# Another planned instruction order for a fused attention and two-layer-pair kernel on one core

## The chip, the cores and the metric

The kernel runs on one core of a Trainium2 chip. The metric is the device time of one execution in microseconds (us). A program that this kernel writes for itself decides at build time in which order each engine's instructions stand; the change gives that program other numbers.

## The reference, cut to what matters

All inputs are drawn at random; attention has 4 batches, 8 heads, 768 steps and a head size of 48, so 3072 tokens of width 384.

```python
def _attn_ref(q, k, v, alpha):
    for t in range(S):
        state = alpha[:, :, t, :, None] * state + np.einsum('bhd,bhe->bhde', k[:, :, t], v[:, :, t])
        y[:, :, t] = np.einsum('bhd,bhde->bhe', q[:, :, t], state)
def _moe_ref(x, w_in, w_out):          # w_in 384x2048, w_out 2048x384
    h = x @ w_in
    g = h * np.cos(h)
    return (g @ w_out).astype(np.float32)
def _moe2_ref(x, w1, w2, w3, w_out):   # w1, w2, w3 384x768, w_out 768x384
    h = np.maximum(np.maximum(x @ w1, x @ w2), x @ w3)
    return (h @ w_out).astype(np.float32)
```

The output is `_moe2_ref` of `_moe_ref` of the attention's result.

## The kernel before

**Tiling.** The 3072 tokens are six units of 512. Every unit goes through attention in four parts (pairs of heads, `k` = 0 to 3), then through the first pair of layers in 16 steps, one for each 128 of the 2048 hidden columns, so 96 steps in all (`moe1(i)`), and, after all units, through the second pair of layers. `att0` is the attention of unit 0, `att` that of units 1 to 5. In `att`, POOL scales k (L505) and q (L508) by running products of alpha that DVE makes with scans (L501, L506); TensorE (PE) transposes k (L513), makes the products of q and k and of k and v (L525, L529), and later the attention's values (L559, L566).

**Products of high and low parts.** PE multiplies fp32r numbers. Each operand is therefore split into a high part and a low part, and each product is three matmuls: L604 to L606 for `x @ w_in` (three such groups in a step, one for each 128 rows of x) and L631 to L633 for `g @ w_out` (three groups, one for each third of the output columns). In a step, ACT and DVE take turns between them: ACT rounds h to a whole number of turns (L612), DVE takes the turns off (L613), ACT takes the sine (L614), DVE multiplies by h (L616 in the first four steps, L620 later), ACT writes the high part (L617, L621), and the low part is a subtraction, on POOL (L618) in the first four steps and on DVE (L626) later. The bank of PSUM that held h is free after the product (first four steps) or after L626. There are five such banks for everything but the three output sums `acc`.

**Weights.** `weight` brings a block of 128x384 weights, stored with 8 bytes each, by a DMA (L344) into one of four buffers `raw` and makes a high and a low part of it: ACT takes the exponents (L345), DVE shifts and joins (L346), ACT writes the high part (L350), and the low part is a subtraction. Where the block's number modulo 4 is in `LOD`, L346 writes a PSUM bank, `raw` is free after it, and DVE subtracts (L352); elsewhere L346 writes back into `raw`, and POOL subtracts (L354). For the first pair of layers even blocks are of `w_in` (tiles `wih`, `wil`), odd ones of `w_out` (`woh`, `wol`); there are 16 of each.

**End of a unit.** The three sums `acc` leave through the one buffer `yy1`, one after the other: ACT copies the high part (L640), DVE subtracts (L641), and a DMA writes both to memory (L643, `x1d`). The copy of the next sum waits until that DMA has landed.

**What sets the order.** Nothing is put into the engines' queues directly. `op` records every step with its engine, an estimated duration, what it reads and writes, and a due number; `Program.order` then plays all engines against each other and, whenever an engine is free, takes the recorded step with the smallest due number among those that it holds to be ready. The due numbers count in steps of the first pair of layers: `moe1(i)`'s matmuls are due at `i`, weights `W1E` steps ahead of their use, their loads `early` before that, attention's part `k` of unit `u` at `16 (u - 1) + ATT0 + ATTS k`. Each engine then executes its queue strictly in that order, SP's queue of DMAs among them. Where the played PE is idle between 7.5 and 45 us, `tile_kernel` fills in matmuls on the identity (L843).

Lines of the planner that the change touches: when a load counts as landed, when its users are ready, and (in `dma_w`) how long weights occupy the DMA:

```python
dma_free = max(dma_free, end + (0.65 if e == "SP" else 1.05)) + nbytes / 295e3
end = dma_free + 0.9
ready_at[u] = max(ready_at[u], end + lag)
return nbytes * 295.0 / 400.0
```

Of the kernel before, what the change touches and what calls it, by code (L numbers as in the profile page):

```python
# [26 lines left out]
P = 128  # L27
C = 64
HB = 512
# [7 lines left out]
KO = AL + 2  # L37
# [6 lines left out]
PR = 112  # L44
# [12 lines left out]
LIMIT = {"h": 3, "a": 3, "t": 2, "w": 1, "r": 2, "y": 2, "r0": 2, "s0": 2}  # L57


RYS = 1  # L60


GLE1 = 0
GLP1 = 4


XLE = 1
MKP = 0
GATE, GSTEP = 1, 3
LOD = (0, 2)  # L70

W1E = 12
MOE_EARLY = 5
EARLY = 3
FIRST = -12
ATT0 = -4.0
ATTS = 3.6


WARM, COLD, IDLE = 2.45, 7.0, 2.5  # L80
# [2 lines left out]
class Program:  # L83
# [38 lines left out]
    def order(self, banks, limit):  # L122
        n = len(self.ops)
        left = [len(o[4]) for o in self.ops]
        users = [[] for _ in range(n)]
        for i, o in enumerate(self.ops):
            for d in o[4]:
                users[d].append(i)
        opens = {}
        bank_of = [[] for _ in range(n)]  # L130
        open_left = {}
        for k, v in self.of_bank.items():
            opens.setdefault(min(v), []).append(k)
            open_left[k] = len(v)
            for i in v:
                bank_of[i].append(k)
        bank_free = [0.0] * banks
        freed_at = {c: [0.0] * limit[c] for c in limit}
        bank_end = {}
        chosen = {}  # L140
        engines = sorted({o[0] for o in self.ops})
        free = dict.fromkeys(engines, 0.8)
        waiting = {e: [] for e in engines}
        ready_at = [0.0] * n
        for i in range(n):
            if not left[i]:
                waiting[self.ops[i][0]].append(i)
        start, ended = [0.0] * n, [0.0] * n
        dma_free = 0.0
        port_free = 0.0  # L150
        cold = COLD
        mode = False
        issued, block, fetched = 0, BLOCK, 0.0
        never = float("inf")

        def single(t):
            return min(range(banks), key=lambda m: (bank_free[m] > t, bank_free[m], m))

        def ready(i):
            t = ready_at[i]  # L160
            need = opens.get(i, ())
            if need:

                t = max(t, sorted(freed_at[need[0][1]])[len(need) - 1], sorted(bank_free)[len(need) - 1])
            if self.ops[i][6]:
                t = max(t, port_free)
            return t

        for _ in range(n):
            _, e, t = min((t - (0.1 if e == "Pool" else 0.0), e, t) for e, t in (  # L170
                (e, max(free[e], min(map(ready, w)))) for e, w in waiting.items() if w))
            assert t < never
            i = min((self.ops[j][5], j) for j in waiting[e] if ready(j) <= t)[1]
            waiting[e].remove(i)
            _, dur, nbytes, _, _, _, port, tiled, count = self.ops[i]
            start[i] = t
            if e == "PE":
                if tiled != mode:
                    dur += SWITCH
                    mode = tiled  # L180
                if t - free[e] > IDLE:
                    cold = t + COLD
                dur += min(dur, max(0.0, cold - t) / 2)
                issued += count
                if issued >= block:
                    late = max(0.0, fetched - t - dur * (1.0 - (issued - block) / count))
                    dur += late
                    fetched = t + dur + (FETCH[1] if dma_free > t + dur else FETCH[0])
                    block += BLOCK
            free[e] = t + dur  # L190
            end = t + dur
            if port:
                port_free = end
            if nbytes is not None:
                dma_free = max(dma_free, end + (0.65 if e == "SP" else 1.05)) + nbytes / 295e3
                end = dma_free + 0.9
            ended[i] = end
            for k in opens.get(i, ()):
                f = min(range(limit[k[1]]), key=lambda f: freed_at[k[1]][f])
                m = single(t)  # L200
                chosen[k] = m
                bank_end[k] = (m, f, 0.0)
                freed_at[k[1]][f] = never
                bank_free[m] = never
            for k in bank_of[i]:
                m, f, last = bank_end[k]
                last = max(last, end + self.SEM)
                bank_end[k] = (m, f, last)
                open_left[k] -= 1
                if not open_left[k]:  # L210
                    freed_at[k[1]][f] = last
                    bank_free[m] = last
            for u in users[i]:
                lag = self.LAG.get((e, self.ops[u][0]), self.SEM)
                ready_at[u] = max(ready_at[u], end + lag)
                left[u] -= 1
                if not left[u]:
                    waiting[self.ops[u][0]].append(u)
        self.start, self.end = start, ended
        return sorted(range(n), key=lambda i: (start[i], i)), chosen  # L220
# [32 lines left out]
def dma(nbytes):  # L253
    return max(nbytes, 15e3)


def dma_w(nbytes):
    return nbytes * 295.0 / 400.0


HW = 0.46


@with_exitstack
def tile_kernel(ctx, tc, aa, qk, vv, wt, outT):
    nc = tc.nc
# [62 lines left out]

    raw_n = [0]  # L330

    def weight(block, hi, lo, whi, wlo, due, extra=(), early=2.0):
        r, tn = (raw_n[0] % NRAW1, raw_n[0] % NTOP) if block < NW1 else (raw_n[0] % NRAW, 0)
        raw_n[0] += 1
        raw, rk, top, tk = raw_b[r], ("raw", r), top_b[tn], ("top", tn)
# [17 lines left out]
        else:  # L353
            op("Pool", pool(WB), lambda: ge.tensor_tensor(lo(), w, hi().bitcast(F32), ALU.subtract), [wk, whi], [wlo], due)  # L354

    def weight1(f, kind, due, early=2.0):
        t = wi if kind == "i" else wo

        def part(n):
            return t[n][:, f].rearrange("p k n -> p (k n)") if kind == "i" else t[n][:, f]  # L360

        weight(2 * f + (kind == "o"), lambda: part("h"), lambda: part("l"), (f"w{kind}h", f), (f"w{kind}l", f), due, early=early)
# [118 lines left out]
    def att(u, k, p, t0):  # L481
        m = u * NP + k
        n2, na, nk, nv = m % 2, m % NIN, m % NKQ, m % NV
        t, kq_, v, kt, a, s, d, z, iv = al_b[na], kq_b[nk], v_b[nv], kt_b[n2], a_b[n2], s_b[p], d_b[n2], z_b[n2], inv0[n2]
        vk, kk_ = ("v", nv), nk
# [6 lines left out]
        kf, kk, kq = ("inf", na), ("ink", kk_), ("inq", kk_)  # L492
# [1 line left out]
        sk = [("s", p, j) for j in range(2)]  # L494
        half = [slice(UP * h, UP * h + D) for h in range(2)]
        first = t0
        op("SP", HW, lambda: nc.sync.dma_start(t, aa[u, p, :, 0:KO]), (), [kf], first - 4.8 + (0.8 if not k else 0), dma(PR * KO * 4))
        op("SP", HW, lambda: nc.sync.dma_start(kq_, qk[u, p]), (), [kk, kq], first - 3.9, dma(PR * 2 * HB * 4))
        op("SP", HW, lambda: nc.sync.dma_start(v, vv[u, p]), (), [vk], first - 3.7, dma(P * HB * 3))
        gate = [("wil", GATE + GSTEP * k)] if u == 1 else []  # L500
        op("DVE", 0.07 + 0.00208 * AL, lambda: ve.tensor_tensor_scan(  # L501
            gf[:, ::-1], t[:, 1:AL + 1][:, ::-1], one0.rearrange("p c t -> p (c t)"), 0.0, ALU.mult, ALU.add), ["one0", kf, *gate], [(*kg, 0), (*kg, 1)], t0 - 1, port=True)
# [49 lines left out]

        yks, y = psum2("r" if u <= RYS else "y")

# [24 lines left out]
        for h in range(2):  # L579
            cs = slice(HB // 2 * h, HB // 2 * (h + 1))  # L580
            first = xa and p == 0 and h == 0
# [232 lines left out]
    start, end = G.start, G.end  # L814
# [9 lines left out]
    for i in order:  # L824
        t = start[i]
# [91 lines left out]
```

## Time and profile before

| | |
|---|---|
| three executions, median (lowest to highest) | 788.72 us (787.69 to 791.11) |
| the profiled execution | 792.77 us |
| its span, first to last instruction | 790.8 us |
| PE busy in the span | 772.0 us |
| DVE, ACT, POOL busy | 427.0, 347.6, 124.3 us |
| granted clock of TensorE, share of full speed | 1.00 |

The profile is of one execution: each instruction with its engine, start and duration, and for an engine that sat idle, what ended the idle time. The durations of neighbouring matmuls overlap, since PE takes the next one up before the last one is through; from start to start a 512-column matmul takes about 0.23 us though each is shown as 0.39. The profiled execution lies 4.05 us above the median of the three others.

### The profile page before, as it was taken

To read this page: it belongs to the slowest core of one execution; us is meant where nothing else is said; L and a number is where in the kernel's file an instruction comes from. 1 tells how busy PE (TensorE), PEld (TensorE's weight loads), DVE (VectorE), ACT (ScalarE), POOL (GpSimd) and SP (SyncE) were. 2 spreads that over 40 slices of the span, in tenths; PEclk is the share of its full clock that TensorE was granted. 3 is DMA by queue.
4 is the path that set the end of the run, shared out by engine and by line. 5 is a ranking of instruction groups with operands and counts; after the bars stand their busy time and mean duration, and the time that the engine had idled before them with its cause. 6 is when DMAs were issued, how large, how long until landed. Compare 5 with 4: busy or idle time off the path is not lost. (4 is left out here: it accounts for less than half of the span.)

```text
span 790.8 us, 14190 instructions
## 1 busy us (share of the span) xinstructions
PE 772.0 (98%) x5863; PEld 625.4 (79%) x5863; DVE 427.0 (54%) x720; ACT 347.6 (44%) x669; POOL 124.3 (16%) x133
## 2 busy tenths in 40 slices
PE   7899899999999999999999999999999999999998
PEld 6677677888888888888878788888888888888886
DVE  8778899756875786566467555532222322223221
ACT  4778756455644554555577444511111212112111
POOL 4463442111111111121133000300000000000000
PEclk9999999999999999999999999999999999999999
DMA  9867735121321133012246300611020200200001
GB/s 276 249 195 205 219 92 164 54 53 47 133 77 29 46 133 94 1 39 107 53 141 225 115 0 2 218 53 42 27 80 27 73 34 28 80 27 14 14 27 41
DMA packets 26464, 69.84 MB, mean 88 GB/s; under 512 B 3392, under 2 KB 6464, under 8 KB 26400
## 3 DMA queue, kind: packets, MB, share of 16 engines
q1 hardware_dynamic: 26400, 68.93, 27.6%
q8 instruction: 46, 0.75, 0.4%
q14 instruction: 18, 0.15, 0.1%
HBM read 52.80 MB, written 14.16 MB: 85 GB/s over the span
## 5 line engine op out<-in xcount | busy, mean ns | idle before, releaser
L631 PE MATMUL acc<-gh,woh 128*128 128x512 f32 x288 | 116.8, 405 | 2.8 <-DVE yy L641 2.4
L604 PE MATMUL ps<-xt,wih 128*128 128x512 f32 x288 | 114.8, 399 | 1.8 <-DVE q L616 1.0
L633 PE MATMUL acc<-gl,woh 128*128 128x512 f32 x288 | 113.1, 393 | 2.5 <-DVE gl L626 2.5
L632 PE MATMUL acc<-gh,wol 128*128 128x512 f32 x288 | 112.5, 391 | 0.0
L606 PE MATMUL ps<-xt,wil 128*128 128x512 f32 x288 | 112.4, 390 | 0.1
L605 PE MATMUL ps<-xt,wih 128*128 128x512 f32 x288 | 112.3, 390 | 0.0
L613 DVE SCALAR_TENSOR_TENSOR q<-q,ps 128x512 f32<-128x512 int32 x96 | 65.4, 682 | 52.5 <-ACT q L612 52.4
L626 DVE TENSOR_TENSOR gl<-ps,gh 128x512 fp32r<-128x512 f32 x92 | 63.2, 687 | 38.5 <-ACT gh L621 38.2
L612 ACT ACTIVATE q<-ps 128x512 int32<-128x512 f32 x96 | 56.8, 595 | 58.5 <-PE ps L606 58.4
L620 DVE TENSOR_TENSOR ps<-q,ps 128x512 f32<-128x512 f32 x92 | 63.6, 691 | 34.8 <-ACT q L614 34.5
L692 DVE TENSOR_TENSOR ps<-t,ps 128x512 f32<-128x512 f32 x36 | 25.1, 696 | 103.5 <-PE ps L684 103.5
L614 ACT ACTIVATE q<-q 128x512 f32<-128x512 f32 x96 | 60.4, 630 | 46.4 <-DVE q L613 46.2
L621 ACT ACTIVATE gh<-ps 128x512 fp32r<-128x512 f32 x92 | 54.7, 594 | 44.3 <-DVE ps L620 38.7
L693 ACT ACTIVATE h<-ps 128x512 fp32r<-128x512 f32 x36 | 21.6, 599 | 108.0 <-DVE ps L692 107.9
L633 PEld LDWEIGHTS acc<-gl,woh 128*128 128x128 f32 x288 | 54.0, 188 | 17.4 <-DVE gl L626 5.4
L631 PEld LDWEIGHTS acc<-gh,woh 128*128 128x128 f32 x288 | 54.0, 188 | 16.2 <-DVE yy L641 3.7
L604 PEld LDWEIGHTS ps<-xt,wih 128*128 128x128 f32 x288 | 54.0, 188 | 14.3 <-DVE q L616 1.1
L606 PEld LDWEIGHTS ps<-xt,wil 128*128 128x128 f32 x288 | 54.1, 188 | 12.3 <-DVE wil L352 0.9
L690 DVE TENSOR_TENSOR t<-t,ps 128x512 f32<-128x512 f32 x36 | 24.8, 688 | 70.4 <-PE ps L684 69.7
L605 PEld LDWEIGHTS ps<-xt,wih 128*128 128x128 f32 x288 | 54.1, 188 | 10.4
L632 PEld LDWEIGHTS acc<-gh,wol 128*128 128x128 f32 x288 | 54.1, 188 | 9.7
L710 ACT ACTIVATE y<-ps 128x512 f32<-128x512 f32 x18 | 10.8, 600 | 93.2 <-PE ps L707 93.2
(147 smaller groups left out, 1425.1 us busy)
## 6 DMA issues: line engine op xcount, KB each, us to landing
raw<-in_wt SPq DMA_DIRECT2D x56, 384.0 KB, 3.9
kq<-in_qk SPq DMA_DIRECT2D x22, 448.0 KB, 4.5
x1d<-yy SPq DMA_DIRECT2D x18, 512.0 KB, 3.4
xt<-x1d SPq DMA_DIRECT2D x18, 512.0 KB, 4.5
al<-in_aa SPq DMA_DIRECT2D x23, 228.4 KB, 2.6
outT<-y SPq DMA_DIRECT2D x18, 256.0 KB, 2.0
v<-in_vv SPq DMA_DIRECT2D x23, 192.0 KB, 4.8
xt<-yy SPq DMA_DIRECT2D x30, 64.0 KB, 3.7
```

The source lines that it names most:

```text
L604: pe.matmul(ps, wi["h"][:, f, cc], xt[:, cc, 0], start=(cc == 0), stop=False)
L605: pe.matmul(ps, wi["h"][:, f, cc], xt[:, cc, 1], start=False, stop=False)
L606: pe.matmul(ps, wi["l"][:, f, cc], xt[:, cc, 0], start=False, stop=(cc == NR - 1))
L612: op("Act", act(HB, True), lambda: se.activation(q.bitcast(I32), ps, AF.Copy, bias=0.25, scale=INV2PI), [hk], [qk, *qx], m)
L613: op("DVE", dve(HB), lambda: ve.scalar_tensor_tensor(q, q.bitcast(I32), -TWOPI, ps, ALU.mult, ALU.add), [hk], [qk], m)
L614: op("Act", act(HB), lambda: se.activation(q, q, AF.Sin, bias=0.5 * math.pi), (), [qk], m)
L620: op("DVE", dve(HB), lambda: ve.tensor_tensor(ps, q, ps, ALU.mult), [qk], [hk], m)
L621: op("Act", act(HB, True), lambda: se.activation(gh, ps, AF.Copy), [hk], [("gh", gn)], m)
L626: op("DVE", dve(HB), lambda: ve.tensor_tensor(gl, ps, gh.bitcast(F32), ALU.subtract), [hk, ("gh", gn)], [("gl", gn)], m)
L631: pe.matmul(acc[c], oh, gh, start=(f == 0), stop=False)
L632: pe.matmul(acc[c], ol, gh, start=False, stop=False)
L633: pe.matmul(acc[c], oh, gl, start=False, stop=(f == NF1 - 1))
```

## The change

The planner's numbers change, and three of its rules. A load counts as landed 1.6 us after its bytes instead of 0.9. A load that `att` issues (alpha, q with k, v) counts as allowed only 5 us after the buffer that it fills is seen free (`SLACK`; the planner knows such loads by `tiled=True`, a mark that DMAs did not carry), so it takes a later place among SP's loads; nothing in the program waits those 5 us. A block of weights counts with its full bytes. The weights of the first pair of layers are due 6 steps ahead of their use instead of 12, their elementwise work and loads also later in terms of due numbers, and attention's parts of units 1 to 5 later and closer together. `LOD` moves DVE's subtraction from PSUM from `w_in` to `w_out`: the low part of `w_in` is now POOL's, that of `w_out` DVE's. `GSTEP` lets unit 1's scans start after other blocks of `w_in`. `XLE` makes the low part of the first three parts of unit 0's attention by a matmul and an ACT copy (L476, L477), where it was only the first; two DVE subtractions (L479) go. `RYS` lets the values of all units share the two banks of the products. The filling matmuls L843 fall away, as the played PE has no such gap any more.

```diff
-RYS = 1
+RYS = 9
...
-XLE = 1
+XLE = 3
 MKP = 0
-GATE, GSTEP = 1, 3
-LOD = (0, 2)
-
-W1E = 12
-MOE_EARLY = 5
-EARLY = 3
-FIRST = -12
-ATT0 = -4.0
-ATTS = 3.6
+GATE, GSTEP = 1, 2
+LOD = (1, 3)
+
+W1E = 6
+MOE_EARLY = 3
+EARLY = 1
+FIRST = -4
+ATT0 = -1
+ATTS = 3.3
...
-                end = dma_free + 0.9
+                end = dma_free + LANDED
...
-                ready_at[u] = max(ready_at[u], end + lag)
+                ready_at[u] = max(ready_at[u], end + lag + (SLACK if self.ops[u][7] and self.ops[u][2] is not None else 0.0))
...
 def dma_w(nbytes):
-    return nbytes * 295.0 / 400.0
-
-
-HW = 0.46
+    return nbytes
+
+
+HW, LANDED, SLACK = 0.46, 1.6, 5.0
...
-    def weight(block, hi, lo, whi, wlo, due, extra=(), early=2.0):
+    def weight(block, hi, lo, whi, wlo, due, extra=(), early=EARLY):
...
-    def weight1(f, kind, due, early=2.0):
+    def weight1(f, kind, due, early=EARLY):
...
-        op("SP", HW, lambda: nc.sync.dma_start(kq_, qk[u, p]), (), [kk, kq], first - 3.9, dma(PR * 2 * HB * 4))
+        op("SP", HW, lambda: nc.sync.dma_start(kq_, qk[u, p]), (), [kk, kq], first - 3.9, dma(PR * 2 * HB * 4), tiled=True)
```

The last line stands for the three loads of `att`.

**PE, around the first L525 of unit 1** (`ident` alone is a filling matmul; `ps_99` to `ps_103` are the five banks). Before, all nine groups L604 to L606 of steps 0 to 2, and the filling, stand ahead of it; from the last group on:

```order
L604 MATMUL ps_99<-xt_324,wih 128x512
L605 MATMUL ps_99<-xt_324,wih 128x512
L606 MATMUL ps_99<-xt_324,wil 128x512
L843 MATMUL ps_102<-ident 128x512
L525 MATMUL ps_100<-kq_104 64x64
```

With the change:

```order
L604 MATMUL ps_102<-xt_326,wih 128x512
L605 MATMUL ps_102<-xt_326,wih 128x512
L606 MATMUL ps_102<-xt_326,wil 128x512
L525 MATMUL ps_103<-kq_104 64x64
L525 MATMUL ps_100<-kq_104 64x64
```

The bank `ps_102` there is step 1's: the three groups of step 2 now follow L525 and L529, and nothing fills.

**DVE, up to the first L626** (the low part of step 4's g; `raw0` to `raw3` and `ps0` to `ps4` are buffers and banks, `wil` and `wol` low parts of weights). Before:

```order
L620 TENSOR_TENSOR ps0_99<-q_82,ps0_99 128x512
L346 SCALAR_TENSOR_TENSOR ps4_103<-raw2_91,top0_93 128x384
L506 SCALAR_TENSOR_TENSOR al2_128<-al2_128,inv1_125 112x520
L352 TENSOR_TENSOR wil_78<-ps4_103,wih_77 128x384
L626 TENSOR_TENSOR gl0_85<-ps0_99,gh0_83 128x512
```

With the change:

```order
L620 TENSOR_TENSOR ps4_103<-q_82,ps4_103 128x512
L346 SCALAR_TENSOR_TENSOR ps3_102<-raw1_90,top1_94 128x384
L346 SCALAR_TENSOR_TENSOR raw2_91<-raw2_91,top0_93 128x384
L626 TENSOR_TENSOR gl0_85<-ps4_103,gh0_83 128x512
L352 TENSOR_TENSOR wol_80<-ps3_102,woh_79 128x384
L613 SCALAR_TENSOR_TENSOR q_82<-q_82,ps1_100 128x512
L506 SCALAR_TENSOR_TENSOR al2_128<-al2_128,inv1_125 112x520
```

The scan L506 and a weight's subtraction L352 stood ahead of L626 and now follow it.

**POOL, around the q of unit 1's last part** (L508; `wol` and `wil` are the low parts of `w_out` and `w_in`). Before:

```order
L354 TENSOR_TENSOR wol<-raw_90,woh 128x384
L539 TENSOR_TENSOR d_112<-s_119,g_130 112x192
L354 TENSOR_TENSOR wol<-raw_92,woh 128x384
L508 TENSOR_TENSOR kq_105<-kq_105,al_127 112x512
L546 COPY kq_105<-kq_105 48x256
```

With the change:

```order
L505 TENSOR_TENSOR kq_105<-kq_105,g_130 112x512
L539 TENSOR_TENSOR d_112<-s_119,g_130 112x192
L508 TENSOR_TENSOR kq_105<-kq_105,al_127 112x512
L354 TENSOR_TENSOR wil<-raw_89,wih 128x384
L546 COPY kq_105<-kq_105 48x256 x2
L354 TENSOR_TENSOR wil<-raw_91,wih 128x384
```

The last two subtractions of weights stood ahead of L508 and now follow it; on DVE the scan L506 that feeds this L508 now stands well ahead of the last L346 of the weights, where it stood behind it.

## Rows read from the trace of the kernel before

**Rows 1.** The page, part 1: busy time of each engine
```profile
PE 772.0 (98%) x5863; PEld 625.4 (79%) x5863; DVE 427.0 (54%) x720; ACT 347.6 (44%) x669; POOL 124.3 (16%) x133
```
**Rows 2.** Stages: width, busy PE, PEld, DVE, ACT, POOL (instructions), clock, DMA share, GB/s
```profile
0.00:26.00 26.00, 21.58 (x182) 16.89 (x183) 21.41 (x46) 14.16 (x36) 14.01 (x23) 1.00 0.96 275
26.00:60.00 34.00, 30.13 (x256) 21.96 (x255) 26.11 (x46) 24.02 (x50) 17.25 (x17) 1.00 0.66 213
60.00:100.00 40.00, 35.96 (x431) 27.52 (x434) 35.76 (x68) 31.45 (x66) 17.64 (x20) 1.00 0.71 205
100.00:140.00 40.00, 39.04 (x565) 30.89 (x556) 38.97 (x69) 23.91 (x49) 13.70 (x14) 1.00 0.43 126
140.00:400.00 260.00, 260.00 (x2757) 211.13 (x2756) 169.98 (x296) 138.85 (x270) 41.17 (x40) 1.00 0.23 68
400.00:440.00 40.00, 38.36 (x166) 30.01 (x165) 28.32 (x46) 30.40 (x59) 14.46 (x14) 1.00 0.61 199
440.00:787.00 347.00, 346.96 (x1531) 286.96 (x1529) 106.49 (x157) 84.25 (x142) 6.12 (x6) 1.00 0.13 47
```
**Rows 3.** PE's timeline: start, duration, instruction [idle before it, ended by]
```profile
25.83 0.39 PE L604 MATMUL ps<-xt,wih 128*128 128x512 f32 x1
...
30.54 0.50 PE L604 MATMUL ps<-xt,wih 128*128 128x512 f32 x1 [0.57 <-ACT wih L350]
...
35.47 1.02 PE L843 MATMUL ps<-ident 128*128 128x512 f32 x2
...
38.80 0.50 PE L604 MATMUL ps<-xt,wih 128*128 128x512 f32 x1 [1.03 <-DVE q L616]
...
59.60 0.51 PE L633 MATMUL acc<-gl,woh 128*128 128x512 f32 x1 [1.52 <-DVE gl L626]
...
80.16 0.50 PE L633 MATMUL acc<-gl,woh 128*128 128x512 f32 x1 [0.99 <-DVE gl L626]
...
99.38 0.69 PE L525 MATMUL ps<-kq 48*64 48x64 f32 x32 [2.25 <-POOL kq L508]
...
135.71 0.50 PE L631 MATMUL acc<-gh,woh 128*128 128x512 f32 x1 [0.96 <-DVE yy L641]
...
437.81 0.50 PE L631 MATMUL acc<-gh,woh 128*128 128x512 f32 x1 [1.46 <-DVE yy L641]
```
**Rows 4.** ACT's and DVE's timeline before the wait that ended at 59.60
```profile
57.39 0.65 ACT L345 ACTIVATE top<-raw 128x384 f16<-128x384 bf16 x1 [1.36 <-DMA raw<-in_wt]
...
58.39 0.56 DVE L352 TENSOR_TENSOR wil<-ps,wih 128x384 fp32r<-128x384 f32 x1 [1.45 <-ACT wih L350]
```
**Rows 5.** DVE's and POOL's timeline before the wait that ended at 99.38
```profile
94.98 0.56 DVE L346 SCALAR_TENSOR_TENSOR raw<-raw,top 128x384 uint32<-128x384 uint32 x1 [1.36 <-ACT top L345]
95.46 1.24 DVE L506 TENSOR_TENSOR_SCAN al<-al,inv 112x520 f32<-112x520 f32 x1
...
97.18 1.01 POOL L354 TENSOR_TENSOR wol<-raw,woh 128x384 fp32r<-128x384 f32 x1 [4.43 <-ACT woh L350]
98.15 1.17 POOL L508 TENSOR_TENSOR kq<-kq,al 112x512 f32<-112x512 f32 x1
```
**Rows 6.** Groups by line: busy us, mean ns | idle before, releasers
```profile
L476 PE MATMUL acc<-yy,gl 128*128 128x512 f32 x1 | 0.5, 487 | 0.0
...
L352 DVE TENSOR_TENSOR wil<-ps,wih 128x384 fp32r<-128x384 f32 x16 | 8.8, 549 | 2.6 <-ACT wih L350 2.4
...
L354 POOL TENSOR_TENSOR wol<-raw,woh 128x384 fp32r<-128x384 f32 x16 | 17.4, 1086 | 28.8 <-ACT woh L350 23.6 <-DMA al<-in_aa 2.4 <-issue 2.2
```
**Rows 7.** The page, part 6: loads of weights, KB each, median us from issue to landing
```profile
raw<-in_wt SPq DMA_DIRECT2D x56, 384.0 KB, 3.9
```
**Rows 8.** One stretch, L604 alone: width, busy PE, PEld (instructions), clock, DMA share, GB/s
```profile
36.00:99.00 63.00, 13.52 (x33) 6.19 (x33) 1.00 0.68 204
```
**Rows 9.** DVE's and POOL's timeline at 46 us
```profile
45.98 1.34 DVE L346 SCALAR_TENSOR_TENSOR ps<-raw,top 128x384 uint32<-128x384 uint32 x1
...
45.87 1.02 POOL L354 TENSOR_TENSOR wol<-raw,woh 128x384 fp32r<-128x384 f32 x1
```

More of the change, by code (lines that the diff above doesn't have):

```diff
@@ L496, in att @@
         first = t0
-        op("SP", HW, lambda: nc.sync.dma_start(t, aa[u, p, :, 0:KO]), (), [kf], first - 4.8 + (0.8 if not k else 0), dma(PR * KO * 4))
-        op("SP", HW, lambda: nc.sync.dma_start(kq_, qk[u, p]), (), [kk, kq], first - 3.9, dma(PR * 2 * HB * 4))
-        op("SP", HW, lambda: nc.sync.dma_start(v, vv[u, p]), (), [vk], first - 3.7, dma(P * HB * 3))
+        op("SP", HW, lambda: nc.sync.dma_start(t, aa[u, p, :, 0:KO]), (), [kf], first - 4.8 + (0.8 if not k else 0), dma(PR * KO * 4), tiled=True)
+        op("SP", HW, lambda: nc.sync.dma_start(kq_, qk[u, p]), (), [kk, kq], first - 3.9, dma(PR * 2 * HB * 4), tiled=True)
+        op("SP", HW, lambda: nc.sync.dma_start(v, vv[u, p]), (), [vk], first - 3.7, dma(P * HB * 3), tiled=True)
         gate = [("wil", GATE + GSTEP * k)] if u == 1 else []
```

## The prediction

> **What bounds the kernel now.** I first read the busy times of the page [rows 1]: PE is busy 772.0 of 790.8 us. The reader is to see two things there. No change of order can win more than the other 18.8 us as long as PE's own work stays, and the 54% of DVE say nothing, since they are a mean over a crowded start and an empty end.
>
> So the second view is busy time by stage [rows 2]. PE's idle time is the width less its busy time: 4.42 us before 26, 3.87 from 26 to 60, 4.04 from 60 to 100, 0.96 from 100 to 140, nothing from 140 to 400, 1.64 from 400 to 440, nothing after; the 3.8 after 787 are the last result's way out. Two stretches, 607 us long, have a full PE whatever the order. Of what a new order can win, 7.9 us lie between 26 and 100, and there DVE and ACT are nearly full too: from 60 to 140 DVE is busy 74.7 of 80 us, PE 75.0. The clock is at its upper level, 2.4 GHz, in every stage, so nothing is to be had from it.
>
> The third view is PE's timeline, for the single waits and what ended each [rows 3]: 0.57 for a weight, 1.03 for a bank that L616 frees, 1.52 and 0.99 for a low part by L626, 2.25 for a q that POOL scales, 0.96 and 1.46 for the end of a unit. Besides, 1.02 us of PE's busy time at 35.47 is filling.
>
> The fourth is the timelines of the engines that were waited for. Before 59.60 ACT waited 1.36 us for a load, and so DVE 1.45 for L352, and L626, which had its inputs, stood behind it [rows 4]. Before 99.38 DVE waited 1.36 us with L346 for a load; the scan L506, which does not need that weight, stood behind, and on POOL L508 stood behind a weight's L354 which had waited 4.43 [rows 5]. Both are work blocked behind a weight's load that it doesn't need.
>
> **The change, part by part.** The sum is made against the profiled execution, 792.77 us, which is 4.05 above the median, 788.72.
>
> *Start, +0.7 us.* PE gets two more L476, 0.49 each as shown [rows 6], 0.23 from start to start, and each then waits for ACT's copy of the high part; DVE loses two subtractions, which PE did not wait for. PE's values of unit 0's first part also move ahead of the second part's products of q and k, and wait there for DVE's masks: in the old order PE had done something else meanwhile. The two L476 alone are 0.46, with nothing beside them on PE; the reordering costs up to one more product of that kind. Bounds 0 and 1.5; I take 0.7, so the first L604 comes at about 26.5 instead of 25.83.
>
> *26 to 60, -3.6 us.* The filling, 1.02, is not emitted. The wait of 0.57 was for step 2's weights; its groups now follow L525 and L529, which give ACT and POOL 0.69 us and more, so it goes. The wait of 1.03 was for step 0's bank: the same chain L612, L613, L614, L616 is left, with about as much PE work beside it, so I count half of it, 0.5. The 1.52 go: L626 stands ahead of L352 and of L506, and behind two L346, whose loads are the ones to watch. The rest of the stage's 3.87, some 0.75 in single waits up to 0.4, I leave as it is. 1.02 + 0.57 + 0.5 + 1.52 = 3.6. Bounds: 4.9 if all of it goes, 2.0 if L626 is then held up by a load in L346.
>
> *60 to 100, -2.25 us.* The long wait goes: L506 stands well ahead of the last L346, and POOL's L508 ahead of the last two L354. Its chain has then no weight in it. The other 1.8 us of the stage I leave: a PE that gets through earlier asks a DVE that has 2.2 us of slack per 20 for the same work, so what is not blocked by a load is late by work. Bounds 0 and 4.04.
>
> *The low part of the weights, 0.* Sixteen times L352, 0.549, leaves the way of `w_in` and L354, 1.086, takes its place; the reverse holds for `w_out` [rows 6]. No engine has more to do. It is 0.54 us more from a load to a ready `wil`, and a buffer `raw` of `w_in` is held through L350 and L354. This is covered while one round of such a buffer (issue to landing 3.9 [rows 7], L345 0.65, L346 0.56, L350 about 0.5, L354 1.09, so 6.7) is shorter than the two steps of PE that it serves. From 36 to 99 us PE began 33 groups with L604, three to a step [rows 8], so a step lasts 63 / 11 = 5.7 us there; 11.4 us stand for the 6.7, and 4.7 are left for queues. If that cover goes, see the second rival.
>
> *End of units, -0.3 us.* The wait at 437.81 has two more groups of L604 to L606 (six starts of 0.23, 1.4 us) ahead of it, but the next sum's copy L640 now stands behind L614 and L612 of later steps, about 1.1 us of ACT. The net is -0.3. At 135.71 there is likewise more PE work ahead, and the first L641 stands behind a scan of attention, 1.24 as in [rows 5]: 0. Bounds for both together: -2.4 and +1.5.
>
> *Later units, 0.* Attention of units 2 to 5 comes later and shares two banks; from 140 to 400 PE is never idle and DVE has 90 us free [rows 2]. If a unit's last part came late, PE would stop at the unit's first L604; in the new order over 30 groups of three matmuls, 0.7 us each, stand between the two.
>
> The sum is 0.7 - 3.6 - 2.25 - 0.3 = -5.45 us: 787.3 for an execution like the profiled one, **783.3 us** for the median. A measurement of this kernel can tell about 0.5% (3.9 us) from no change; this is 0.7%.
>
> **A rule weighed.** At 45.98 a DVE L346 took 1.34 us; POOL's L354 had begun at 45.87 and ran 1.02 [rows 9]. The same operation takes 0.56 where POOL is idle [rows 5]. So a collision costs 0.78 here.
>
> The Trainium skill, SBUF — State Buffer, section "SBUF: two separate sides", says that VectorE and GpSimd hold one port pair as an exclusive lock, so that an operation of VectorE with two SBUF inputs waits for the whole of GpSimd's. The trace agrees: that L346 ended 0.43 us after the L354 did. By the rule a new order that lays L354 and L346 side by side more often loses 0.78 us each time, which is the third rival below.
>
> **The rivals.**
>
> *DVE or the loads bound the start.* For it: from 60 to 140 DVE has as much to do as PE, and DMAs are busy 96% before 26 and 66 to 71% up to 100 [rows 2]. Then what the order frees comes back as other waits of the same engines, L626 late by work or by another load. Against it: the waits named were blocked by loads that the waiting work did not need. It keeps the filling and the half of the long wait, 1.02 + 1.1, less 0.7 at the start: -1.4, 787.3 us.
>
> *`wil` becomes the last to come (slower).* L354 stands in POOL's queue among L505, L508 and L539, and the weights are due six steps later, so there is less store of ready ones. It decides where a round of a `w_in` buffer passes the 11.4 us of two steps, that is, where its 6.7 meet more than 4.7 us of queues; waits of L354 of 4.43 occur [rows 5]. Its price is then the 0.54 in each of steps 4 to 15, 12 x 0.54 = 6.5 us, with none of the waits removed but the filling's 1.02 and with the 0.7 at the start: 788.7 + 6.5 - 0.3, 795 us.
>
> *The port.* The 16 L354 move among more scans and L346. If eight of them collide anew, 8 x 0.78 = 6.2 us of DVE, where DVE has no slack: against the -5.45 it leaves +0.8, 789.5 us. Against it: there are as many L354 as before, and such collisions are in the trace already.
>
> *The order hardly matters.* PE's rows are nearly the same; if the same loads are late in the same places, the time is 788.7 within 1.5 us. Against it: the two places where the order is what blocked [rows 4, 5].
>
> **How the numbers follow.** Forecast 0.57 (778.8 to 785.6), DVE or loads 0.21 (785 to 788.7), `wil` 0.11 (790 to 797), the port 0.05, order indifferent 0.06. The lower end of the forecast is the sum with the better bounds in part (-4.9, -4.04 and -1 for the ends of units: -9.9, 778.8); its own upper end has 2.0 and 1.5 in place of 3.6 and 2.25 (-3.1, 785.6). Leaving out most of `wil` and a little on both sides gives 778.5 to 790. Faster by over 0.5% (under 784.8) takes nearly all of the forecast: 0.55. Slower by over 0.5% (above 792.7) is `wil` and a little of the rest: 0.11. Within 0.5%: 0.34.
>
> **What would show it.** Right: PE's idle time from 26 to 100 falls from 7.9 to about 4 us, no L843, no wait above 1 us at the first L633 of step 4 nor at unit 1's last L525, the first L604 at 26 to 27, and the stretches from 140 on as long as before. DVE's rivalry would show as new waits of PE for L626 or L620 between 60 and 140 with DVE above 95% busy; `wil` as waits of L606 or L604 for POOL's L354; the port as L346 or L506 of 1.2 to 2 us beside L354. I am wrong if PE's idle time by stage stays and the time falls all the same, or if units 2 to 5 show idle PE.

## The result, and the profile after

The changed kernel takes 780.73 us (median of 4 runs, 780.38 to 781.45), the kernel before 789.72 in the same measurement (4 runs, 787.69 to 791.11): a ratio of 0.989, 95% interval 0.987 to 0.991, so 9.0 us faster, 1.1%. The prediction was 783.3 in 778.5 to 790. The profiled execution took 780.58 us, close to its median; that of before, at 792.77, lay 3 us above its own. From profile to profile the difference is therefore 12.1 us of span (790.8 to 778.7), while the medians give the change 9.0.

The page, part 1, of the changed kernel answers to [rows 1]:

```profile
PE 768.0 (99%) x5863; PEld 627.5 (81%) x5863; DVE 425.1 (55%) x718; ACT 348.4 (45%) x671; POOL 127.3 (16%) x133
```

The stages of the changed kernel, with the columns of [rows 2]:

```profile
0.00:26.00 26.00, 22.83 (x188) 18.39 (x189) 21.96 (x47) 14.58 (x37) 15.14 (x24) 1.00 0.97 286
26.00:60.00 34.00, 32.22 (x332) 25.43 (x331) 29.15 (x51) 27.69 (x57) 20.20 (x20) 1.00 0.66 211
60.00:100.00 40.00, 40.00 (x478) 32.38 (x477) 38.67 (x74) 32.35 (x68) 18.68 (x21) 1.00 0.68 209
100.00:140.00 40.00, 39.02 (x469) 31.16 (x467) 34.41 (x62) 23.33 (x48) 9.76 (x10) 1.00 0.36 112
140.00:400.00 260.00, 259.03 (x2754) 210.88 (x2753) 170.75 (x296) 139.06 (x269) 42.98 (x40) 1.00 0.23 68
400.00:440.00 40.00, 39.96 (x175) 32.31 (x174) 28.35 (x46) 30.80 (x58) 14.45 (x14) 1.00 0.66 227
```

PE's timeline of the changed kernel: the rows that answer to [rows 3], with every wait of 0.2 us or more after 26 us but one (0.97 at 358.69, told below under later units):

```profile
24.75 0.40 PE L604 MATMUL ps<-xt,wih 128*128 128x512 f32 x1
...
30.30 0.50 PE L604 MATMUL ps<-xt,wih 128*128 128x512 f32 x1 [0.77 <-ACT xt L474]
31.58 0.50 PE L605 MATMUL ps<-xt,wih 128*128 128x512 f32 x1 [0.78 <-DVE xt L479]
34.22 0.50 PE L604 MATMUL ps<-xt,wih 128*128 128x512 f32 x1 [0.23 <-DVE wol L352]
36.40 0.39 PE L604 MATMUL ps<-xt,wih 128*128 128x512 f32 x1
...
124.41 0.50 PE L631 MATMUL acc<-gh,woh 128*128 128x512 f32 x1 [0.98 <-DVE yy L641]
```

What to see in the stages: PE's idle time is 3.17 us before 26 (4.42 before), 1.78 from 26 to 60 (3.87), nothing from 60 to 100 (4.04), and 0.04 from 400 to 440 (1.64). Between 34.3 and 124 us no wait of PE stands on the timeline at all. Against that, 0.97 is new between 140 and 400. Idle time falls by 8.0 us in all (sum of the stages), and PE's *busy* time falls too, from 772.0 to 768.0, of which the filling L843 is 1.0.

One line of the waits of ACT carries the explanation to which the runs lead. It gives the engine, what it waited for, the total in us, the number of waits and the longest one. Before:

```profile
ACT top L345 <- DMA raw<-in_wt: 15.0, 18, 2.5
```

and with the change:

```profile
ACT top L345 <- DMA raw<-in_wt: 4.8, 5, 1.5
```

L345 is the first of a weight block's operations. Before, ACT reached eighteen of them ahead of the block's load and stood still for 15.0 us in all, with everything behind them in its queue; now five, for 4.8 us.

### The profile page after: what moved, and what is told of

The parts are those of the page before. It is cut to its first block, busy times and chain, and to the rows that moved or that the text cites. A ratio compares the mean times of both kernels' runs of the same rounds, so it can differ in the third digit from the quotient of the medians.

```text
span 778.7 us, 14199 instructions
## 1 busy us (share of the span) xinstructions
PE 768.0 (99%) x5863; PEld 627.5 (81%) x5863; DVE 425.1 (55%) x718; ACT 348.4 (45%) x671; POOL 127.3 (16%) x133
## 4 chain that ended last, share of the span: by engine, by line
PE 94%; DMA 3%; ACT 1%; DVE 1%; issue 0%; POOL 0%; SPq 0%; ACTq 0%; POOLq 0%; DVEq 0%
PE ps L682 9%; PE ps L683 9%; PE ps L684 9%; PE acc L631 9%; PE ps L604 8%; PE acc L633 8%; PE acc L632 8%; PE ps L605 8%; PE ps L606 8%; PE ps L705 3%; PE ps L707 3%; PE ps L706 3%; PE ps L525 2%; PE ps L559 1%; DMA raw<-in_wt 1%; PE ps L566 1%
## 5 line engine op out<-in xcount | busy, mean ns | idle before, releaser
L631 PE MATMUL acc<-gh,woh 128*128 128x512 f32 x288 | 116.0, 403 | 1.0 <-DVE yy L641 1.0
L604 PE MATMUL ps<-xt,wih 128*128 128x512 f32 x288 | 114.7, 398 | 1.0 <-ACT xt L474 0.8
L633 PE MATMUL acc<-gl,woh 128*128 128x512 f32 x288 | 112.2, 390 | 0.0
L606 PE MATMUL ps<-xt,wil 128*128 128x512 f32 x288 | 112.1, 389 | 0.0
L613 DVE SCALAR_TENSOR_TENSOR q<-q,ps 128x512 f32<-128x512 int32 x96 | 65.6, 683 | 46.9 <-ACT q L612 46.8
L620 DVE TENSOR_TENSOR ps<-q,ps 128x512 f32<-128x512 f32 x92 | 63.7, 692 | 35.8 <-ACT q L614 35.7
L626 DVE TENSOR_TENSOR gl<-ps,gh 128x512 fp32r<-128x512 f32 x92 | 62.9, 687 | 35.6 <-ACT gh L621 35.0
L614 ACT ACTIVATE q<-q 128x512 f32<-128x512 f32 x96 | 60.6, 631 | 39.7 <-DVE q L613 39.4
L621 ACT ACTIVATE gh<-ps 128x512 fp32r<-128x512 f32 x92 | 54.8, 597 | 47.4 <-DVE ps L620 44.0
L631 PEld LDWEIGHTS acc<-gh,woh 128*128 128x128 f32 x288 | 54.0, 188 | 13.5 <-DVE yy L641 1.6
L604 PEld LDWEIGHTS ps<-xt,wih 128*128 128x128 f32 x288 | 54.1, 188 | 13.0 <-ACT xt L474 1.2
L633 PEld LDWEIGHTS acc<-gl,woh 128*128 128x128 f32 x288 | 54.1, 188 | 12.0 <-DVE gl L626 0.4
L606 PEld LDWEIGHTS ps<-xt,wil 128*128 128x128 f32 x288 | 54.1, 188 | 11.4
```

The lines of the kernel that those rows point to most:

```text
L604: pe.matmul(ps, wi["h"][:, f, cc], xt[:, cc, 0], start=(cc == 0), stop=False)
L606: pe.matmul(ps, wi["l"][:, f, cc], xt[:, cc, 0], start=False, stop=(cc == NR - 1))
L613: op("DVE", dve(HB), lambda: ve.scalar_tensor_tensor(q, q.bitcast(I32), -TWOPI, ps, ALU.mult, ALU.add), [hk], [qk], m)
L620: op("DVE", dve(HB), lambda: ve.tensor_tensor(ps, q, ps, ALU.mult), [qk], [hk], m)
L626: op("DVE", dve(HB), lambda: ve.tensor_tensor(gl, ps, gh.bitcast(F32), ALU.subtract), [hk, ("gh", gn)], [("gl", gn)], m)
L631: pe.matmul(acc[c], oh, gh, start=(f == 0), stop=False)
```

## The experiments

Each kernel was timed against the kernel before on the same chip; before's median lay between 789.2 and 790.5 us beside them. The changed kernel was timed only once, in the first measurement, so a difference to it of up to 1 us says nothing. The waits of L345 are those of the one profiled execution.

| kernel | median (us) | ratio to before, 95% | waits of L345 for a load (us, times) |
|---|---|---|---|
| before | 789.72 | | 15.0, 18 |
| the change | 780.73 | 0.987 to 0.991 | 4.8, 5 |
| before, three operations moved | 790.88 | 0.999 to 1.003 | 14.6, 16 |
| change, loads planned as before | 791.34 | 1.000 to 1.004 | 13.6, 12 |
| change, weights due 12 steps ahead | 785.71 | 0.993 to 0.997 | 6.8, 9 |
| change, low parts as before | 783.11 | 0.989 to 0.994 | 4.2, 4 |
| before, new rules on loads alone | 784.16 | 0.990 to 0.994 | 9.9, 9 |
| change, no hold on attention's loads | 784.26 | 0.991 to 0.994 | 6.1, 6 |
| change, landing and bytes as before | 787.36 | 0.996 to 0.998 | 14.0, 14 |
| change, end of unit 0 moved | 780.47 | 0.986 to 0.990 | 4.2, 5 |
| change, twelve L345 earlier | 793.14 | 1.002 to 1.005 | 13.2, 11 |
| change, longer landing, hold of 8 us | 793.94 | 1.004 to 1.008 | 4.2, 7 |
| change, attention due as before | 782.29 | 0.988 to 0.993 | 5.1, 5 |
| change, eight L345 earlier | 789.81 | 0.998 to 1.002 | 12.8, 10 |

**The named waits, undone by hand.** In the kernel before, L626 of step 4 goes ahead of L506 and L352, unit 1's last L506 ahead of the last L346, and L508 ahead of the last L354; nothing else.

```diff
+    for i, j in ((400, 294), (434, 259), (435, 261)):
+        order.remove(i)
+        order.insert(order.index(j), i)
```

> The order of before with three steps moved by hand and nothing else: DVE's L626 of step 4 ahead of the scan L506 and the weight's L352, DVE's scan L506 of unit 1's last part ahead of the last L346, POOL's L508 of that part ahead of the last L354. Theory (work blocked behind a weight's load): PE's waits of 1.52 us at the first L633 of step 4 and of 2.25 us at unit 1's last L525 both fall below 0.5 us, and the time falls by 2.5 to 3.8 us. Rival (DVE's work is the bound): the waits come back as others of PE between 60 and 140, and the time falls by 0 to 1.5 us.

790.88 us against 789.62: no gain, or by the interval 0.7 us at most, where 2.5 to 3.8 were expected. The waits for L626 and L508 that were named are gone, but PE's timeline of this run has others in their place:

```profile
61.28 0.69 PE L525 MATMUL ps<-kq 48*64 48x64 f32 x32 [1.25 <-POOL kq L508]
64.85 0.49 PE L604 MATMUL ps<-xt,wih 128*128 128x512 f32 x1 [0.93 <-DVE wil L352]
```

So the two places on which the largest terms of the prediction rested do not make the time. ACT's waits at L345 are hardly touched (14.6 us). PE's idle time from 26 to 100 us is lower in this one profile, 4.9 us against 7.9, but the profile of before is of an execution 3 us above its median, and in this one PE was late at the start already (first L604 at 28.20), with the granted clock at its lower level from 14.35 to 17.76 us.

**The loads' rules taken back.**

```diff
-HW, LANDED, SLACK = 0.46, 1.6, 5.0
+HW, LANDED, SLACK = 0.46, 0.9, 0.0
...
-    return nbytes
+    return nbytes * 295.0 / 400.0
```

> The changed kernel with the planner's three old rules on loads (landing 0.9, no hold on attention's loads, weights at 295/400 of their bytes). If the gain rests on the planner knowing the loads, most of it goes: 4 to 9 us slower than the changed kernel, with new waits of PE behind L345's or L346's wait for a load. If it rests on the due numbers and the low parts, 0 to 2 us slower.

791.34 us, 10.6 more than the change: with the three rules on loads gone, the whole gain is gone, though due times, low parts and the start are those of the change. ACT waits 13.6 us at L345 again. PE stood for 2.54 us until 38.39, for a bank that L616 frees.

**Due times and low parts taken back**, one at a time.

```diff
-W1E = 6
+W1E = 12
...
-EARLY = 1
+EARLY = 2.0
```

> The changed kernel with weights due 12 steps ahead and their loads 2 ahead, as before. Theory (weights that are not yet needed stood ahead of what PE waits for): 3 to 7 us slower than the changed kernel, PE idle from 26 to 100 again 4 us or more. Rival (the low parts or the rules on loads did it): within 1.5 us of the changed kernel.

785.71 us, 5.0 more than the change; L508 is waited for again (1.12 us before 60.13).

```diff
-LOD = (1, 3)
+LOD = (0, 2)
```

> The changed kernel with the low part of w_in on DVE from PSUM and that of w_out on POOL, as before. Rival (a buffer of w_out is free earlier, so loads flow earlier): 2 to 6 us slower than the changed kernel. Theory (the sum counts this as 0): within 1.5 us of it.

783.11 us, 2.4 more than the change; the intervals of the two ratios overlap, the times of the two kernels do not. ACT's waits are as short as with the change (4.2 us), and so the low parts seem to have an effect of another kind: PE waits 1.57 us before 37.63 for a bank that L616 frees. The parts are not additive: the three taken back cost 10.6, 5.0 and 2.4 us, 18.0 together, twice the change's 9.0.

**The loads' rules alone**, in the kernel before (the lines of the second run the other way round, and `tiled=True` on attention's loads). This expectation and three below describe the rule `SLACK` wrongly: it is no distance between a load's landing and its first user, but keeps attention's own loads back by 5 us in the plan.

> The kernel before with the three rules on loads alone (a load's landing planned 0.7 us later, the whole of a weight's bytes on the wire, 5 us between a landing and its first user, attention's loads under the same rule); due times, low parts, products of the start and attention's times as before. New theory, from the traces of the four runs so far: what the change wins is ACT's waits at a weight's L345 for its load, since everything in ACT's and DVE's order stands behind them. They were 15.0 us in 18 waits before, 14.6 in 16 with three operations moved by hand, 13.6 in 12 with the loads planned as before, and 4.8 in 5 with the whole change. It expects here 4 to 8 us of such waits and a time of 782 to 785.5, since due times and low parts measured 5.0 and 2.4 us. Rival (the rules need the new due times and attention's new times to have room): waits of L345 above 10 us and a time of 788 to 791. My first theory, which counted single waits of TensorE, has no reason for a gain beyond the waits at L633 and L525, about 3.8 us: 785 to 787.

784.16 us, 5.4 less than before (789.51 beside it): the rules give six tenths of the gain by themselves. The time is as the new theory expected, though only 0.8 us below the range of the first theory, and the waits (9.9 us in 9) lie above the new theory's 4 to 8.

**The two halves of the loads' rules.** First `SLACK = 0.0` alone, then `LANDED = 0.9` and 295/400 of the bytes with the 5 us kept.

> The changed kernel without the 5 us that the planner puts between a load's landing and its first user (0 in their place); landing and bytes as changed. If this distance is what takes L345 out of the way of loads that are late, ACT's waits at L345 come back above 10 us and the time is 788 to 791. If the longer landing and the whole bytes carry it, the waits stay at 4 to 7 us and the time at 781 to 783.

> The changed kernel with the load's own price as before (0.9 us to land, 295/400 of a weight's bytes), and the 5 us to the first user kept. The mirror of the run without the 5 us: if the distance carries the gain, 781 to 783 with ACT's waits at L345 at 4 to 7 us; if the price of the load carries it, 786 to 791 with waits above 10 us. If both runs lose less than half of the 10.6 us that the three rules together were worth, either one is enough.

784.26 and 787.36 us: the hold on attention's loads is worth 3.5, the price of a load 6.6, and both together 10.6. The first time lies between the two ranges expected, the second in the range for the price. The waits go the same way, 6.1 and 14.0 us. Most of it is thus in the longer price of a load, by which the planner puts L345 further from its load's issue; neither half is enough alone.

**Twelve L345 earlier.** In the changed kernel twelve L345 between 34 and 62 us were moved ahead by hand.

```diff
+    for i, j in ((49, 295), (59, 297), (64, 317), (69, 359), (74, 361), (79, 71),
+                 (84, 288), (89, 335), (94, 381), (99, 385), (104, 423), (109, 345)):
+        order.remove(i)
+        order.insert(order.index(j), i)
```

> The changed kernel with nothing but ACT's order touched: twelve of the L345 between 34 and 62 us stand one to four operations earlier, each at a place that in the profile of the changed kernel came 0.4 to 1.5 us before its load landed; loads, DVE, POOL and TensorE keep their order. If ACT's waits at L345 are the cause, they rise from 4.8 us to some 10 to 15 and the time to 784 to 788, more than half of the way back, with new waits of TensorE for L621, L616 and L626 between 40 and 70 us. Rival (those waits are only a sign of late loads, and ACT, which is busy 27.7 of 34 us there, has the time for them): the waits rise as said and the time stays at 780.5 to 782.

793.14 us. It doesn't decide: nine of the twelve ran ahead of the L346 that had still to read the same scratch `top`, so nine weights' lower bits were taken from another block, and those L346 waited for the later load besides. The run that is told last was made in its place.

**More of the same.** `LANDED = 2.2` and `SLACK = 8.0`.

> The changed kernel with more of the same: a landing planned at 2.2 us in place of 1.6, and 8 us to the first user in place of 5. If the remaining 4.8 us of waits at L345 are worth what the first ten were, they fall below 3 us and the time to 778.5 to 780. Rival (what is left of idle time is at the start, 3.2 us before 26, which waits for work and not for loads; longer distances only put weights later): 780.5 to 784, with new waits of TensorE for a weight's L354 or L352.

793.94 us, 13.2 more than the change and above both ranges, with ACT's waits as short as there (4.2 us). Few waits at L345 are thus not enough. The waits of SP's queue and of PE in this kernel:

```profile
SPq L344 <- POOL wil L354: 35.8, 12, 12.0
```

```profile
PE acc L631 <- DVE yy L641: 7.6, 5, 3.2
```

SP stood once for 12.0 us (36.3 to 48.4) at a weight's load whose buffer POOL's L354 had to free, where the longest such wait with the change is 3.7; but PE has no wait of 0.2 us or more between 38 and 72 us, so it isn't shown that this stall costs the time. What PE lost stands elsewhere: it waited 7.6 us at the ends of units, where it was 1.0, and its idle time is 8.0 us more in all. Part of the longest of these waits is once more work behind a weight, the copy L640 behind an L350 on ACT:

```profile
442.98 0.55 ACT L350 ACTIVATE w1h<-raw 128x384 fp32r<-128x384 f32 x1 [1.01 <-DVE raw L346]
443.42 0.58 ACT L640 ACTIVATE yy<-acc 128x512 fp32r<-128x512 f32 x1
```

Why the other ends of units came late was not followed, and which of the two numbers does it wasn't tried.

**Attention's times taken back.**

```diff
-FIRST = -4
-ATT0 = -1
-ATTS = 3.3
+FIRST = -12
+ATT0 = -4.0
+ATTS = 3.6
```

> The changed kernel with attention's due times as before (its first part 12 steps ahead of its use in place of 4, its later parts earlier and spread a little wider). If attention's operations come ahead of the feed-forward's again, the scans L506 and L501 stand in DVE's way between 40 and 100 us: 783 to 786, with waits of TensorE for L626 or L620 there. Rival (the planner places attention by its inputs and the due times hardly matter once the weights are due later): 780.5 to 782.

782.29 us, 1.6 more than the change, a little above the rival's range and below the other's. Before took 790.54 beside it, so measured against that about 1 us of the gain is lost, and the intervals of the two ratios overlap: if the due times of attention matter, then least of the parts tried.

**The end of unit 0 moved**, in the changed kernel: L640 and L641 of the third sum ahead of L549 and L551.

```diff
+    for i, j in ((598, 656), (599, 657)):
+        order.remove(i)
+        order.insert(order.index(j), i)
```

> The changed kernel with the end of unit 0 moved by hand: the third copy L640 ahead of L549 and L614 on ACT, and its L641 ahead of L551 and the scan L501 on DVE. TensorE waited 0.98 us at 124.41 for that L641, which stood behind a scan of 1.23 us. If the wait is blocked work, it falls to under 0.3 us and the time by 0.6 to 1.0, to 779.7 to 780.2. Rival (the scan, 0.67 us later, is late itself for the next unit's L513 and L525, or TensorE gives the time back at the next unit's end): 780.5 to 781.5, with a new wait of 0.5 us or more between 125 and 140.

780.47 us (779.91 to 782.78): not told apart from 780.73. The wait of 0.98 us is gone, and another stands behind it:

```profile
127.58 0.50 PE L633 MATMUL acc<-gl,woh 128*128 128x512 f32 x1 [0.37 <-DVE gl L626]
```

No version that is shown to be faster than the change came out of these runs.

**Eight L345 earlier, and nothing else.**

```diff
+    for i, j in ((29, 281), (49, 295), (69, 361), (79, 71),
+                 (109, 104), (119, 437), (139, 489), (154, 146)):
+        order.remove(i)
+        order.insert(order.index(j), i)
```

> The changed kernel with eight L345 of ACT (of the weights' blocks 4, 8, 12, 14, 20, 22, 26 and 29) one to four operations earlier, each at a place where, in the profile of the changed kernel, its load lands 0.6 to 1.8 us later while the scratch that it writes is already free. Nothing else moves on any engine, and no L346 depends on another copy than before, as it did in the run with twelve moves (nine of those twelve ran ahead of the L346 that still had to read the same scratch, so a weight's low bits were taken from another weight and that L346 waited for the later load besides). ACT's waits at L345 for a load should rise by about 9 us, to 12 to 15. If these waits are the cause, half or more of the 8.8 us come back: 785 to 790. Rival (they are a sign of late loads, and ACT has 6 of 34 us free from 26 to 60 and 7.6 of 40 from 60 to 100): 780.5 to 782. In between, 782 to 785, each microsecond of such a wait costs a part of itself, and the rest of the gain is the loads' own order.

789.81 us against 789.19 for before: the whole gain is gone. ACT's waits are 12.8 us, 8.0 more than with the change, and the time is 9.1 more. Every other queue has the order of the change, and on ACT only the places of eight operations of 0.65 us differ. The stages from 26 to 100 us:

```profile
26.00:60.00 34.00, 29.41 (x257) 22.36 (x256) 24.33 (x43) 24.76 (x50) 17.40 (x17) 1.00 0.61 192
60.00:100.00 40.00, 38.03 (x454) 28.98 (x453) 33.15 (x64) 28.50 (x59) 17.39 (x18) 0.96 0.63 189
```

PE's idle time is back (4.59 and 1.97 us), while ACT and DVE do *less* than with the change. The mean clock of the twelve executions is 0.9976, so some 1.9 of the 9.1 us are TensorE's clock (an estimate; see the last section). How one such wait travels is to be read from the timelines of this run, ACT, DVE and PE:

```profile
34.52 0.55 ACT L350 ACTIVATE wih<-raw 128x384 fp32r<-128x384 f32 x1
36.96 0.63 ACT L345 ACTIVATE top<-raw 128x384 f16<-128x384 bf16 x1 [1.89 <-DMA raw<-in_wt]
37.47 0.60 ACT L614 ACTIVATE q<-q 128x512 f32<-128x512 f32 x1
...
34.00 0.68 DVE L613 SCALAR_TENSOR_TENSOR q<-q,ps 128x512 f32<-128x512 int32 x1
...
38.10 0.69 DVE L616 TENSOR_TENSOR q<-q,ps 128x512 f32<-128x512 f32 x1 [2.02 <-ACT q L614]
...
37.16 0.39 PE L606 MATMUL ps<-xt,wil 128*128 128x512 f32 x1
38.84 0.50 PE L604 MATMUL ps<-xt,wih 128*128 128x512 f32 x1 [1.30 <-DVE q L616]
```

The same place in the timelines of the changed kernel, ACT and PE:

```profile
34.14 0.63 ACT L614 ACTIVATE q<-q 128x512 f32<-128x512 f32 x1
34.66 0.66 ACT L345 ACTIVATE top<-raw 128x384 f16<-128x384 bf16 x1
...
36.40 0.39 PE L604 MATMUL ps<-xt,wih 128*128 128x512 f32 x1
```

The sine L614 had its input when this L613 ended at 34.68, and ACT was free at 35.07. But L614 stood behind an L345 that waited for its load until 36.96; so L616 came 2 us late, so the bank came free late, and PE's first L604 of step 3 came at 38.84 instead of 36.40 (1.45 us by this wait, the rest by an earlier one that ended at 35.20). The profile puts PE's wait down to DVE's L616, two engines away from the load. That ACT takes its work strictly in the order of its queue is also what the Trainium skill says (PSUM — Partial Sum Buffer, section "Engine vs sequencer instructions": the queues of these engines are strict FIFO); the trace agrees, with 1.89 us, from 35.07 to 36.96, in which L614 was ready and ACT did nothing. A second one is plainer still. L621 had had its input since DVE's L620 ended at 71.61 and stood behind an L345 that came at 73.02, and the clock fell behind PE's wait (last section):

```profile
73.02 0.63 ACT L345 ACTIVATE top<-raw 128x384 f16<-128x384 bf16 x1 [0.92 <-DMA raw<-in_wt]
73.52 0.57 ACT L621 ACTIVATE gh<-ps 128x512 fp32r<-128x512 f32 x1
...
74.14 0.50 PE L631 MATMUL acc<-gh,woh 128*128 128x512 f32 x1 [1.18 <-ACT gh L621]
```

So it is the wait, and not only the earlier place of a 0.65 us operation, that held up these two. Not every new wait of PE was followed back in this way.

## Why the prediction was right, and where its sizes were off

The sign and the range held; the likeliest time was 2.6 us too high, with a sum of -5.45 where the medians differ by 9.0 and the profiles by 12.1. The kind of mechanism, work that stands behind a weight's load that it doesn't need, is shown by the last run. Its place was wrong, and that the sum came as near as it did is in good part luck: more than half of its two largest terms are the waits of 1.52 and 2.25 us, whose removal by hand won nothing. How much of the 9.0 us is ACT's ten fewer us of waits isn't separated either: kernels with 4.2 us of them took from 780.5 to 793.9.

**26 to 60 (-3.6) and 60 to 100 (-2.25).** Idle time fell by 2.09 and 4.04 us and the filling's 1.02 went, so -3.11 and -4.04 from profile to profile. Of the single waits before 60 the 0.57, 1.03 and 1.52 are all gone, and two of 0.77 and 0.78 for `xt` are new. But the step by which the two terms were worked out failed: "The 1.52 go: L626 stands ahead of L352 and of L506" and "The long wait goes: L506 stands well ahead of the last L346". Both waits went in the run with three operations moved, and the time did not fall. I had read in [rows 4] that ACT waited 1.36 us at L345, and counted the one operation behind DVE's part of it. The line of ACT's waits, 15.0 us in 18, was there to be read and was not: I followed PE's waits one by one to the engine they name, and the load stands two engines behind that name.

"The other 1.8 us of the stage I leave ... what is not blocked by a load is late by work" is where 60 to 100 went wrong: nothing of it was late by work. DVE does 38.67 us in those 40 now, more than the 35.76 of [rows 2], and PE doesn't wait.

**Start (+0.7).** The first L604 came at 24.75, 1.1 us earlier, not 0.7 later. With the kernel before's products at the start and the new loads' rules it came at 25.38, and with the change's products in runs with other orders behind them at 24.88 to 25.55 (clock at its upper level throughout the start); so the two more L476 cost nothing that can be seen, and part of the 1.1 us is the scatter of single profiles.

**Low parts (0).** Not nothing: about 2.4 us are lost without this part. The cover that I named (rounds of `raw` shorter than two steps) seems to hold, since no wait for `wil` is left on PE's timeline of the changed kernel; why the old choice costs a wait for L616 before 37.63 was not followed further.

**Ends of units (-0.3).** +0.02 at unit 0 (0.96 to 0.98) and -1.60 for the unit that ends after 400 us, where no wait is left. **Later units (0).** +0.97: one L525 of attention waited for ACT's L516. Idle PE in units 2 to 5 was one of the prediction's own signs of being wrong; it came, though small.

**What no term held.** The sum of these, with -1.25 us of idle time before 26, is -9.0 from profile to profile. The other 3.0 are in PE's busy time: 772.0 to 768.0, less the filling. My sentence that no order can win more than the 18.8 us of idle time was wrong by this. A wait costs more than is shown in brackets: above, 37.16 to 38.84 is 1.68 us from start to start, where 0.23 would be usual; 1.45 lost for a wait of 1.30. Summed over L604 to L606 and L631 to L633, such hidden time falls by 0.9 us (nine waits to three), and what is lost in starts that stand over 0.26 us apart with no wait shown falls by another 1.6; that is 2.5 of the 3.0.

**The rivals.** *The order hardly matters* and *the loads bound the start* fall with the time. *`wil` last to come* did not occur. *The port* did not either: the 31 L346 between 26 and 140 took 19.0 us together, 19.4 before. Eight of them were lengthened by a POOL operation before and six now; each of these ended 0.41 to 0.43 us after that operation, so a collision cost 0.1 to 0.8 us by when it began. "Nothing is to be had from the clock" [rows 2] was too much said; see below.

## What to carry to other kernels

Where engines take their work in a fixed order, look up for each engine what it waits for at the head of its queue, before following the waits of the busiest engine one by one: a wait for a DMA on an engine with 20% of its time free cost about its own length on PE, under another engine's name (8.0 us of waits, 9.1 of time, the clock included). How long a planner takes its loads to be is then worth tuning in both directions: with the three old rules the kernel lost 10.6 us, with a longer landing and a longer hold 13.2, the latter without more waits at L345 and for a reason that is only in part known. An undone wait proves a cause only when it is undone alone: moving just three operations gave nothing, moving just eight copies took everything away.

## What the runs showed that was not expected

PE's granted clock fell to its lower level, 1.2 GHz, behind waits of 0.7 to 3.2 us. In the run with the eight L345, PE stood for 0.70 and 1.18 us between 70 and 74.6, and then:

```profile
70.00:74.60 4.60, 2.72 (x11) 1.00 0.67 198
74.60:78.10 3.50, 3.50 (x10) 0.51 0.61 155
78.10:82.00 3.90, 3.90 (x24) 1.00 0.74 235
```

(Columns: stretch, width, busy PE with its instructions, granted clock as a share of 2.4 GHz, DMA share, GB/s.) For 3.4 us the clock was at 1.2 GHz; neighbouring matmuls started 0.43 us apart there (75.46 to 75.89) and 0.23 elsewhere, so about half of it is lost, 1.7 us. In the run with the loads planned as before it fell in the same way at 38.58, behind the wait of 2.54 us that ended at 38.39, and at 134.15, behind one of 2.53 that ended at 132.74. The length of a wait alone doesn't decide it: behind the 2.25 us of [rows 3] that ended at 99.38 the clock stayed up, and with the longer landing it fell at 38.50 behind 1.28 us.

Neither profile of before and after has such a stretch, but every execution comes with its mean clock, and one such stretch takes 0.002 off the mean (half of 3.4 us in 790). Of 79 executions of the kernel before beside these runs, 38 have a mean of 0.998 or less and took 790.8 us on average; the other 41 took 788.9. Of 41 executions of the change and of the six variants that stay under 786 us, none has. So about 1 us of the 9.0 is the clock that is not lost (an estimate), and with it a part of the scatter: before runs from 786.9 to 793.9, and still to 791.7 where its mean clock is 0.999 or more; the change runs from 780.4 to 781.5. In the run with the eight L345 the mean is 0.0024 short of 1, which stands for 1.9 us of 790. That the waits bring the clock down is argued from where the stretches lie, not shown by a run that changes only that.
